# Narrowing a float64 weight tile by tile: w_out of block 0 by itself, and w_out two blocks behind gate and val

## The chip, the cores and the metric

The kernel runs on one core of a Trainium2 chip. The metric is the time of one execution on the device in microseconds, as the median of three executions. Every time below is in microseconds (us), unless it is marked ns.

## The reference

Two stages stand one behind the other. The first is an attention with a polynomial sketch, for 4 batches of 4 heads with 1088 tokens of 32 values. Its output, 4352 tokens of 128 values, is the input of a gated feed-forward layer.

```python
def phi(x):                                   # S1, S2: 8 x 32
    a = np.einsum('rd,bhsd->bhsr', S1, x)
    b = np.einsum('rd,bhsd->bhsr', S2, x)
    return np.einsum('bhsi,bhsj->bhsij', a, b).reshape(*x.shape[:-1], r * r)
q_p, k_p = (phi(q), phi(k))
kv = np.einsum('bhsf,bhsd->bhfd', k_p, v)
z = np.sum(k_p, axis=2)
num = np.einsum('bhsf,bhfd->bhsd', q_p, kv)
den = np.einsum('bhsf,bhf->bhs', q_p, z)[..., None] + 1e-06
attn = num / den
...                                           # x: (4352, 128), from attn
gate = 1.0 / (1.0 + np.exp(-(x @ w_gate)))    # w_gate, w_val: 128 x 1536
val = x @ w_val
out = (gate * val) @ w_out                    # w_out: 1536 x 128
```

S1, S2, w_gate, w_val and w_out reach the kernel as 64-bit floats; q, k and v are 32-bit floats.

## The kernel before

The hidden size of 1536 is worked in 12 blocks of 128 (`NJ = 12`), and the tokens in 9 chunks (eight of 512 and one of 256). For each chunk and block TensorE makes a *wave* (gate and val of the block, two products), ScalarE the sigmoid `sg`, VectorE the product `g`, and TensorE adds `w_out.T @ g` of the block into `moeout`. The products of w_out run two blocks behind the waves.

TensorE takes 32-bit floats, so each 64-bit weight is *narrowed* first. It arrives as two 32-bit words, and one part of the weights goes through four steps that are shared out over three engines, each step being called by its number (0 to 3) from where it is wanted in the program:

```python
def narrow(out, bits, eng, bank=None, copies=None):
    ...
    # step 0: GpSimd (eng) and ScalarE read the raw words
    eng.tensor_scalar(out=cap.bitcast(F32), in0=hi.bitcast(F32), scalar1=122880.0, scalar2=-122880.0,
                      op0=ALU.min, op1=ALU.max)
    nc.scalar.activation(out=tail, in_=lo, func=ACTF.Copy, scale=2.0**-29)
    yield
    # step 1: VectorE, two instructions
    nc.vector.tensor_scalar(out=head, in0=cap, ...)
    nc.vector.scalar_tensor_tensor(out=head, in0=cap, ..., in1=head, ...)
    yield
    # step 2: ScalarE and GpSimd
    square = ...                      # in a bank of PSUM ("acc0" or "acc1"), or over cap
    nc.scalar.activation(out=square, in_=cap.bitcast(F32), func=ACTF.Square)
    nc.gpsimd.tensor_tensor(out=head, in0=head, in1=tail, op=ALU.add)
    yield
    # step 3: VectorE writes the 32-bit weights
    nc.vector.scalar_tensor_tensor(out=out, in0=square, ..., in1=head, op0=ALU.is_ge, op1=MUL)
    yield
```

The raw words come in by loads on SyncE's queue, all of them issued at the head of the program, in this order and with the loads of q and v between:

```python
load_w_in(0, 1)                       # gate and val of block 0
v_t[0] = load_v(0)
load_w_in(1, 2)                       # gate and val of block 1
load_w_out(0)                         # w_out of blocks 0 and 1
load_rows(q, 0, q_t[0], ((T0, T, nc.sync),))
for n in range(1, NJ // 2):
    load_w_in(2 * n, 2 * n + 2)       # gate, then val, of blocks 2n and 2n+1
    load_w_out(n)                     # w_out of blocks 2n and 2n+1
```

The raw words of each pair of blocks have a tile of their own (`raw` has six of them, `[P, 3, 2, P, 2]`: gate, val, w_out; two blocks; 128 weights; two words). The parts are: gate and val of block 0; gate and val of block 1; w_out of blocks 0 and 1; and from block 2 on gate, val and w_out of one block together.

```python
for part in range(2):
    narrow_01(part, 0)                # gate and val of blocks 0 and 1: step 0
...
def rest(turn, rc, dT):               # on the way to the first tokens x
    kv0([1, 2, 3, 4, 0])
    ...
    turn()
    nc.scalar.activation(out=rc[:, :nt], in_=dT[:, :nt, :2], func=ACTF.Identity, bias=eps)
    kvd(0)
    narrow_01(0, 1)
    narrow_01(0, 2)
    ndt(0)
divide = dn(0, 0, rest)
warm(256)                             # products of constants, of no use but to keep TensorE at work
def head1():
    narrow_01(1, 1)
    narrow_01(0, 3)
    narrow_01(1, 2)
    narrow_01(2, 0)                   # w_out of blocks 0 and 1
    narrow_w(2, 0)                    # gate, val and w_out of block 2
divide((0, 4), (4, 8), between=head1)
narrow_01(1, 3)
narrow_01(2, 1)
narrow_01(2, 2)
```

The rest of the parts is called from within the waves of the first chunk (`ci == 0`), two blocks ahead:

```python
nc.scalar.activation(out=sg, in_=wv[:, 0], func=ACTF.Sigmoid)
if ci == 0:
    if j0 == 1:
        narrow_01(2, 3)
    if 0 < j0 < NJ - 2:
        narrow_w(j0 + 1, 3)
    narrow_w(j0 + 2, 1)
    narrow_w(j0 + 2, 2)
    if j0 < 3:
        narrow_w(j0 + 3, 0)
    if j0 > 1:
        narrow_w(j0 + 4, 0)
```

In the loop over the waves the product of w_out of block j - 2 stands right ahead of wave j:

```python
while len(todo) >= lag:               # lag is 2
    w2(*todo.pop(0))                  # moeout += w_out.T @ g, of block j - 2
if more:
    w1()                              # the wave of block j
```

Of the kernel before, what the change touches and what calls it, by code (L numbers as in the profile page):

```python
# [8 lines left out]
F32 = mybir.dt.float32  # L9
I32 = mybir.dt.int32  # L10
# [6 lines left out]
P = 128  # L17
# [3 lines left out]
def kernel(  # L21
# [12 lines left out]
    nc = tc.nc  # L34
# [6 lines left out]
    NJ = DFF // P  # L41
# [10 lines left out]
    const = ctx.enter_context(tc.tile_pool(name="const", bufs=1))  # L52
    ld = ctx.enter_context(tc.tile_pool(name="ld", bufs=1))
    sbA = ctx.enter_context(tc.tile_pool(name="sbA", bufs=2))
    raw = ctx.enter_context(tc.tile_pool(name="raw", bufs=NJ // 2))
    sbN = ctx.enter_context(tc.tile_pool(name="sbN", bufs=1))
    sbG = ctx.enter_context(tc.tile_pool(name="sbG", bufs=6))

# [21 lines left out]
    wide = S1.dtype == I64  # L80
# [61 lines left out]
                nc.sync.dma_start(out=rows, in_=s_)  # L142


    w_sb = const.tile([P, 3, NJ, P], F32, tag="w_sb", name="w_sb")
    w_in = {}

    def load_w_in(j0, j1):
        cs = slice(j0 * P, j1 * P)
        n, jj = divmod(j0, 2)  # L150
        if wide and jj == 0:
            w_in[n] = raw.tile([P, 3, 2, P, 2], I32, tag="w_in", name="w_in")
        for i, src in enumerate((moe_w_gate, moe_w_val)):
            if wide:
                nc.sync.dma_start(  # L155
                    out=w_in[n][:, i, jj : jj + j1 - j0].rearrange("p j m w -> p (j m w)"),
                    in_=src[:, cs].bitcast(I32),
                )
            else:
                nc.sync.dma_start(  # L160
                    out=w_sb[:, i, j0:j1].rearrange("p j m -> p (j m)"), in_=src[:, cs]
                )

    def load_w_out(n):
        j0, j1 = 2 * n, 2 * n + 2
        cs = slice(j0 * P, j1 * P)
        src = moe_w_out[cs, :].bitcast(I32) if wide else moe_w_out[cs, :]
        nc.sync.dma_start(
            out=w_in[n][:, 2].rearrange("p j m w -> p j (m w)") if wide else w_sb[:, 2, j0:j1],
            in_=src.rearrange("(j p) m -> p j m", p=P),  # L170
        )

    narrowing = {}

    def narrow_w(j, step):
        if not 0 <= j < NJ:
            return
        n, jj = divmod(j, 2)
        if wide:
            if step == 0:  # L180
                narrowing[j] = narrow(
                    w_sb[:, :, j, :], w_in[n][:, :, jj], nc.gpsimd, "acc1" if j < NJ - 2 else None
                )
            next(narrowing[j])


    def narrow_01(part, step):
        if wide:
            if step == 0:
                i = (slice(0, 2), part) if part < 2 else (2, slice(0, 2))  # L190
                narrowing["01", part] = narrow(
                    w_sb[:, i[0], i[1]],
                    w_in[0][:, i[0], i[1]],
                    nc.gpsimd,
                    "acc0" if part else "acc1",
                )
            next(narrowing["01", part])


    def load_rows(src, b, t, parts=((0, T, nc.sync),)):  # L200
# [76 lines left out]
    for c in range(2):  # L277
        rows = slice(64 * c, 64 * c + 64)
        nc.vector.tensor_reduce(
            out=m_col[rows, c],  # L280
            in_=ident[rows].rearrange("p (k j) -> p j k", j=R),
# [3 lines left out]
    for t, x in (  # L285
# [5 lines left out]
        out=e_sum,  # L291
        in_=bass.AP(
            tensor=e_row.tensor,
            offset=e_row.offset,
            ap=[list(e_row.ap[0]), [0, 2], [1, R], [0, R]],
        ),
# [13 lines left out]
    def w2(ci, j0, jn, g):  # L310
        t0, tw = tok_chk[ci]
        if j0 == 0:
            moe["sum"] = ci
            moe["acc"] = pso.tile([P, TCH], F32, tag=f"acc{ci % 2}", name="moeout")
        for jj in range(jn):
            j = j0 + jj
            nc.tensor.matmul(  # L317
                out=moe["acc"][:, :tw],
                lhsT=w_sb[:, 2, j, :],
                rhs=g[:, jj, :tw],  # L320
                start=(j == 0),
                stop=(j == NJ - 1),
            )
        if j0 + jn == NJ:
            o_sb = sbA.tile([P, TCH // 32, 32], F32, tag="o_sb", name="o_sb")
            nt = tw // 32
            nc.vector.transpose(  # L327
                out=o_sb[:, :nt, :].rearrange("p t d -> p (t d)"), in_=moe["acc"][:, :tw]
            )
            c = t0  # L330
            while c < t0 + tw:
                b, r = divmod(c, S)
                n = min(t0 + tw - c, S - r) // 32
                u = (c - t0) // 32
                for g4 in range(4):
# [12 lines left out]
    def w1():  # L348

        ci = moe["ci"]  # L350
        t0, tw = tok_chk[ci]
        jn = TCH // tw
        j0 = moe["w"] * jn
        wv = psm.tile([P, 2, TCH], F32, tag="wave", name="wave")

        tp = tw // 2 if ci == 0 and j0 == 0 else tw
        for o in range(0, tw, tp):
            for which in range(2):
                for jj in range(jn):
                    nc.tensor.matmul(  # L360
                        out=wv[:, which, jj * tw + o : jj * tw + o + tp],
                        lhsT=w_sb[:, which, j0 + jj, :],
                        rhs=xT[:, t0 + o : t0 + o + tp],
                        start=True,
                        stop=True,
                    )
        sg = sbG.tile([P, TCH], F32, tag="sg", name="sg", bufs=3)
        nc.scalar.activation(out=sg, in_=wv[:, 0], func=ACTF.Sigmoid)  # L368
        if ci == 0:
            if j0 == 1:  # L370
                narrow_01(2, 3)
            if 0 < j0 < NJ - 2:
                narrow_w(j0 + 1, 3)
            narrow_w(j0 + 2, 1)
            narrow_w(j0 + 2, 2)
            if j0 < 3:
                narrow_w(j0 + 3, 0)
            if j0 > 1:
                narrow_w(j0 + 4, 0)


        def glu():
            g = sbG.tile([P, TCH], F32, tag="g", name="g")
            nc.vector.tensor_tensor(out=g, in0=wv[:, 1], in1=sg, op=MUL)  # L384
            moe["todo"].append((ci, j0, jn, g.rearrange("p (j t) -> p j t", j=jn)))

        moe["gate"] = glu
        moe["w"] += 1
        if j0 + jn == NJ:
            moe["ci"] += 1  # L390
            moe["w"] = 0
# [140 lines left out]
    def outer(b, pi, j0=0, j1=NJK, eng=nc.vector):  # L532
        a0 = KAB[b][:, pi, j0:j1]
        ap = [list(a0.ap[0]), [2 * R, 2 * (j1 - j0)]]
        eng.tensor_tensor(  # L535
            out=KP[b][:, pi, j0:j1].rearrange("p j m (i l) -> p (j m) i l", i=R),
            in0=bass.AP(tensor=a0.tensor, offset=a0.offset, ap=ap + [[1, R], [0, R]]),
            in1=bass.AP(tensor=a0.tensor, offset=a0.offset + R, ap=ap + [[0, R], [1, R]]),
            op=MUL,
        )  # L540
# [257 lines left out]
    else:  # L798
        nc.vector.tensor_copy(
            out=s4[:, 1:],  # L800
            in_=bass.AP(
                tensor=s4.tensor, offset=s4.offset, ap=[list(s4.ap[0]), [0, 3], [1, D]]
            ),
# [5 lines left out]
        out=st_[:, : 2 * R],  # L809
        lhsT=s4.rearrange("p g d -> p (g d)"),  # L810
# [9 lines left out]
        out=sk,  # L820
# [13 lines left out]
    for n, inner in enumerate(([[1, R], [0, R]], [[0, R], [1, R]])):  # L834
# [3 lines left out]
            out=t, in_=bass.AP(tensor=s0.tensor, offset=s0.offset, ap=[list(s0.ap[0])] + inner)  # L838
# [9 lines left out]
    mult10 = ab(None, (0, 1, 0), (psm, "wave"))  # L848
    for pi in range(2):
        outer(0, pi, NJK - 1, NJK, eng=nc.gpsimd)  # L850
    for part in range(2):
        narrow_01(part, 0)
    spread_z()
    warm(512)
    for pi in range(2):
# [6 lines left out]
    def rest(turn, rc, dT):  # L862
        kv0([1, 2, 3, 4, 0])
        for pi in range(2):
            outer(0, pi, 5, NJK - 1)
        kv0(range(5, NJK))
        turn()
        nt = rc.shape[1] - 1
        nc.scalar.activation(out=rc[:, :nt], in_=dT[:, :nt, :2], func=ACTF.Identity, bias=eps)
        kvd(0)  # L870
        narrow_01(0, 1)
        narrow_01(0, 2)
        ndt(0)

    divide = dn(0, 0, rest)
    warm(256)

    def head1():
        narrow_01(1, 1)
        narrow_01(0, 3)  # L880
        narrow_01(1, 2)
        narrow_01(2, 0)
        narrow_w(2, 0)

    divide((0, 4), (4, 8), between=head1)
    narrow_01(1, 3)
    narrow_01(2, 1)
    narrow_01(2, 2)

    slot(None, 1)  # L890
    cq = {}
# [82 lines left out]
```

## Time and profile before

The median is 305.58 us, of executions between 305.27 and 306.23. The profiled execution has a span of 303.6 us at a granted TensorE clock of 0.998. By stage:

| stretch, us | what runs | TensorE busy, us | VectorE | ScalarE | GpSimd | DMA, GB/s |
|---|---|---|---|---|---|---|
| 0 to 15.20 | attention of the first tokens | 13.14 | 12.38 | 6.61 | 4.93 | 286 |
| 15.20 to 50.57 | first chunk, parts 2 to 11 narrowed | 34.86 | 30.44 | 16.77 | 17.04 | 146 |
| 50.57 to 283.50 | the other chunks, attention between | 232.93 | 106.27 | 54.02 | 13.33 | 57 |
| 283.50 to 303.60 | last chunks, output | 16.41 | 5.73 | 3.58 | 0.00 | 21 |

How to read the profile's lines: `PE` is TensorE's products and `PEld` its loads of weights, `DVE` is VectorE, `ACT` ScalarE, `POOL` GpSimd and `SP` SyncE; a `q` behind an engine's name is its queue, which issues and waits. `L127` is line 127 of the kernel, and `w_sb<-square,head` reads: written from. Several lines of the profile are lines of helpers: L97 and L101 are step 0 of a narrowing (`cap` and `tail`), L105 and L109 step 1 (`head`), L117 and L118 step 2 (`square`, and the add into `head`), L127 step 3 (`w_sb`). L360 is the wave, L317 the product of w_out, L155 the load of w_gate and w_val, L168 that of w_out. An end of a product is modelled: back to back, one of 512 columns has a pass every 0.429 us, and its record is some 0.16 us longer.

### The profile page before, as it was taken

How to read it: one execution, taken by the hardware profiler on the slowest of the kernel's cores; microseconds unless marked ns; L12 is line 12 of the kernel's file. 1: busy time of each engine (PE TensorE's matmuls, PEld its weight loads, DVE VectorE, ACT ScalarE, POOL GpSimd, SP SyncE). 2: the span in 40 equal slices, each digit the busy share in tenths (PEclk: the TensorE clock that was granted, in tenths of full speed). 3: DMA queues.
4: the chain of work that ended last, by engine and by line, in shares of the span. 5: the costliest groups of instructions: out<-in, count | busy, mean ns of one | idle time of the engine just before them, and what ended most of it. 6: DMA issues, size and time to landing. Idle time of an engine off the chain costs nothing.

```text
span 303.6 us, 3618 instructions
## 1 busy us (share of the span) xinstructions
PE 297.3 (98%) x1366; PEld 136.9 (45%) x1366; DVE 154.8 (51%) x266; ACT 81.0 (27%) x150; POOL 35.3 (12%) x65
## 2 busy tenths in 40 slices
PE   8899999999999999999999999999999999999995
PEld 3444433454344444433444445334444444444683
DVE  6997788756556444464365443635232223222331
ACT  2556532221222222221222222221222222222220
POOL 1465540600000500000005000000000000000000
PEclk9999999999999999999999999999999999999999
DMA  7992440897202593440016930200010000100011
GB/s 219 354 341 68 124 144 6 174 182 181 74 9 56 92 174 56 94 169 0 0 18 129 174 64 2 36 2 0 0 23 11 0 0 9 28 0 0 7 31 17
DMA packets 29874, 23.31 MB, mean 77 GB/s; under 512 B 20960, under 2 KB 25056, under 8 KB 29856
## 3 DMA queue, kind: packets, MB, share of 16 engines
q1 hardware_dynamic: 25488, 15.21, 18.5%
q0 software_dynamic: 3456, 7.09, 13.6%
q10 hardware_dynamic: 912, 0.77, 0.9%
q8 instruction: 11, 0.18, 0.2%
q14 instruction: 7, 0.06, 0.1%
HBM read 19.80 MB, written 3.26 MB: 76 GB/s over the span
## 4 chain that ended last, share of the span: by engine, by line
PE 84%; DMA 7%; DVE 4%; POOL 3%; issue 1%; SPq 1%; ACT 0%; POOLq 0%; ACTq 0%
PE wave L360 52%; PE moeout L317 27%; DMA v<-in_v_dram 3%; POOL head L118 3%; DMA w_in<-in_moe_w_out_dram 2%; DMA w_in<-in_moe_w_gate_dram 2%; DVE w_sb L127 1%; DVE head L109 1%; PE kvz L657 1%; PE nps L754 1%; PE dps L735 1%; DVE head L105 1%; PE kps L456 1%; PE cqps L602 0%; SPq L155 0%
## 5 line engine op out<-in xcount | busy, mean ns | idle before, releaser
L360 PE MATMUL wave<-xT,w_sb 128*128 128x512 f32 (+1 forms) x436 | 191.7, 565 | 0.1
L384 DVE TENSOR_TENSOR g<-wave,sg 128x512 f32<-128x512 f32 x102 | 70.3, 689 | 130.1 <-ACT sg L368 129.8
L360 PEld LDWEIGHTS wave<-xT,w_sb 128*128 128x128 f32 x436 | 82.6, 190 | 93.6 <-issue 86.3
L368 ACT ACTIVATE sg<-wave 128x512 f32<-128x512 f32 x102 | 60.9, 597 | 199.0 <-PE wave L360 199.0
L317 PE MATMUL moeout<-g,w_sb 128*128 128x512 f32 (+1 forms) x216 | 105.4, 576 | 0.3 <-DVE w_sb L127 0.3
L317 PEld LDWEIGHTS moeout<-g,w_sb 128*128 128x128 f32 x216 | 39.5, 190 | 43.9 <-issue 37.1
L626 POOL DMA_DIRECT2D qp<-dq x12 | 7.1, 590 | 109.1 <-DMA dq<-cq 67.5
L118 POOL TENSOR_TENSOR head<-head,tail 128x384 int32<-128x384 int32 (+2 forms) x14 | 13.4, 954 | 17.8 <-DVE head L109 14.7
L535 DVE TENSOR_TENSOR kp<-kab 128x1152 f32<-128x1152 f32 (+2 forms) x10 | 10.5, 1069 | 0.0
L635 DVE TENSOR_TENSOR qp<-qp,bq 128x1152 f32<-128x1152 f32 (+1 forms) x7 | 9.1, 1293 | 1.1 <-DMA bq<-dq 1.1
L258 PE MATMUL warm<-const-float32-1.0 128*128 128x512 f32 (+1 forms) x12 | 7.2, 724 | 0.8 <-PEq L958 0.8
L109 DVE SCALAR_TENSOR_TENSOR head<-cap,head 128x384 int32<-128x384 int32 (+2 forms) x14 | 7.5, 535 | 0.5
L127 DVE SCALAR_TENSOR_TENSOR w_sb<-square,head 128x384 f32<-128x384 f32 (+1 forms) x11 | 5.7, 518 | 3.9 <-POOL head L118 3.9
L327 DVE STREAM_TRANSPOSE o_sb<-moeout 128x512 f32<-128x512 f32 (+1 forms) x9 | 6.1, 680 | 2.6 <-PE moeout L317 2.5
L626 POOL DMA_DIRECT2D bq<-dq x12 | 7.0, 579 | 0.3
L101 ACT ACTIVATE tail<-w_in 128x384 int32<-128x384 uint32 (+1 forms) x13 | 6.5, 517 | 0.5 <-DMA w_in<-in_moe_w_gate_dram 0.5
L97 POOL TENSOR_SCALAR cap<-w_in 128x384 f32<-128x384 f32 (+1 forms) x13 | 6.5, 504 | 0.0
L781 DVE TENSOR_TENSOR xT<-nps,rb 128x576 f32<-128x576 f32 (+2 forms) x9 | 5.9, 661 | 0.7
L770 DVE STREAM_TRANSPOSE rb<-rc 128x576 f32<-128x576 f32 (+2 forms) x9 | 6.1, 680 | 0.3
L754 PE MATMUL nps<-qp,nd 64*32 64x256 f32 (+1 forms) x128 | 5.5, 401 | 0.4 <-ACT nd L726 0.4
L439 DVE STREAM_TRANSPOSE qT<-kq 128x512 f32<-128x512 f32 (+1 forms) x8 | 5.7, 718 | 0.0
L117 ACT ACTIVATE square<-cap 128x384 f32<-128x384 f32 (+1 forms) x11 | 5.1, 463 | 1.9 <-DVE w_sb L127 1.8
(73 smaller groups left out, 84.6 us busy)
## 6 DMA issues: line engine op xcount, KB each, us to landing
qp<-dq POOLq DMA_DIRECT2D x12, 288.0 KB, 9.3
bq<-dq POOLq DMA_DIRECT2D x12, 288.0 KB, 9.6
v<-in_v_dram SPq DMA_DIRECT2D x16, 144.0 KB, 6.1
kq<-in_k_dram SPq DMA_DIRECT2D x3, 544.0 KB, 4.0
kq<-in_q_dram SPq DMA_DIRECT2D x3, 544.0 KB, 4.9
w_in<-in_moe_w_out_dram SPq DMA_DIRECT2D x6, 256.0 KB, 6.9
w_in<-in_moe_w_gate_dram SPq DMA_DIRECT2D x5, 256.0 KB, 5.7
w_in<-in_moe_w_val_dram SPq DMA_DIRECT2D x5, 256.0 KB, 4.8
```

Source lines behind the costliest of these rows:

```text
L109: nc.vector.scalar_tensor_tensor(out=head, in0=cap, scalar=-0x40000000, in1=head, op0=ALU.bitwise_and, op1=ALU.bitwise_or)
L118: nc.gpsimd.tensor_tensor(out=head, in0=head, in1=tail, op=ALU.add)
L127: nc.vector.scalar_tensor_tensor(out=out, in0=square, scalar=1.265625 * 2.0**-30, in1=head, op0=ALU.is_ge, op1=MUL)
L258: nc.tensor.matmul(out=t[:, 0, :n], lhsT=x, rhs=r, start=True, stop=True)
L317: nc.tensor.matmul(out=moe["acc"][:, :tw], lhsT=w_sb[:, 2, j, :], rhs=g[:, jj, :tw], start=(j == 0), stop=(j == NJ - 1),)
L360: nc.tensor.matmul(out=wv[:, which, jj * tw + o : jj * tw + o + tp], lhsT=w_sb[:, which, j0 + jj, :], rhs=xT[:, t0 + o : t0 + o + tp], sta ...
L368: nc.scalar.activation(out=sg, in_=wv[:, 0], func=ACTF.Sigmoid)
L384: nc.vector.tensor_tensor(out=g, in0=wv[:, 1], in1=sg, op=MUL)
L535: eng.tensor_tensor(out=KP[b][:, pi, j0:j1].rearrange("p j m (i l) -> p (j m) i l", i=R), in0=bass.AP(tensor=a0.tensor, offset=a0.offset, ...
L626: get.dma_start(out=t[64 * c : 64 * c + 64, n * H * W1 : (n + 1) * H * W1], in_=bass.AP(tensor=d0.tensor, offset=d0.offset, ap=rows + [[1, ...
L635: nc.vector.tensor_tensor(out=q0, in0=q0, in1=half(BQ[b], n), op=MUL)
L754: nc.tensor.matmul(out=t[32 * h : 32 * h + 32, c, :w], lhsT=ND[b][rows, 32 * h : 32 * h + 32], rhs=half(QP[b], n)[rows, 2 * (h % 2) + h // ...
```

## The change

The change aims at the first products of w_out: they need only w_out of block 0, but that is narrowed together with w_out of block 1, and gate and val of block 2 together with a w_out that is not needed until later. So w_out of block 0, and gate and val of block 2, become parts of their own; from block 3 on a part holds gate and val of block j with w_out of block j - 2; and one last part holds w_out of blocks 10 and 11. For a part to be one access with a fixed step, the raw words of all blocks lie in one tile: gate of blocks 0 to 11 on places 0 to 11, val on 12 to 23, two empty places, and w_out on 26 to 37. A part of block j takes places j, j + 12 and j + 24. The 32-bit weights `w_sb` lie in the same way. Loads, their order and their sizes stay.

```diff
-    raw = ctx.enter_context(tc.tile_pool(name="raw", bufs=NJ // 2))
+    raw = ctx.enter_context(tc.tile_pool(name="raw", bufs=1))
...
-    w_sb = const.tile([P, 3, NJ, P], F32, tag="w_sb", name="w_sb")
-    w_in = {}
+    w_sb = const.tile([P, 3 * NJ + 2, P], F32, tag="w_sb", name="w_sb")
+    w_in = raw.tile([P, 3 * NJ + 2, P, 2], I32, tag="w_in", name="w_in") if wide else None
...
-                    out=w_in[n][:, i, jj : jj + j1 - j0].rearrange("p j m w -> p (j m w)"),
+                    out=w_in[:, i * NJ + j0 : i * NJ + j1].rearrange("p j m w -> p (j m w)"),
...
+        to = slice(2 * NJ + 2 + j0, 2 * NJ + 2 + j1)
...
-            out=w_in[n][:, 2].rearrange("p j m w -> p j (m w)") if wide else w_sb[:, 2, j0:j1],
+            out=w_in[:, to].rearrange("p j m w -> p j (m w)") if wide else w_sb[:, to],
...
+    def narrow_w(part, step):
+        if wide and part in places:
             if step == 0:
-                narrowing[j] = narrow(
-                    w_sb[:, :, j, :], w_in[n][:, :, jj], nc.gpsimd, "acc1" if j < NJ - 2 else None
-                )
...
+                at, bank = places[part]
+                narrowing[part] = narrow(w_sb[:, at], w_in[:, at], nc.gpsimd, bank)
+            next(narrowing[part])
+
+    places = {j: (slice(j, j + 2 * NJ + 1, NJ), "acc1") for j in range(3, NJ - 2)}
+    places.update({j: (slice(j, j + 2 * NJ + 1, NJ), None) for j in range(NJ - 2, NJ)})
+    places.update({("gv", j): (slice(j, j + NJ + 1, NJ), f"acc{1 - j % 2}") for j in range(3)})
+    places["out", 0] = slice(2 * NJ + 2, 2 * NJ + 3), "acc0"
+    places[NJ] = slice(3 * NJ, 3 * NJ + 2), None
...
-                lhsT=w_sb[:, 2, j, :],
+                lhsT=w_sb[:, 2 * NJ + 2 + j, :],
...
         if ci == 0:
-            if j0 == 1:
-                narrow_01(2, 3)
-            if 0 < j0 < NJ - 2:
-                narrow_w(j0 + 1, 3)
-            narrow_w(j0 + 2, 1)
-            narrow_w(j0 + 2, 2)
+            if j0 == 0:
+                narrow_w(("gv", 2), 1)
+                narrow_w(("gv", 2), 2)
+                narrow_w(("out", 0), 3)
+            else:
+                if j0 == 1:
+                    narrow_w(("gv", 2), 3)
+                elif j0 != NJ - 2:
+                    narrow_w(j0 + 1, 3)
+                narrow_w(j0 + 2, 1)
+                narrow_w(j0 + 2, 2)
...
     def head1():
-        narrow_01(1, 1)
-        narrow_01(0, 3)
-        narrow_01(1, 2)
-        narrow_01(2, 0)
-        narrow_w(2, 0)
+        narrow_w(("gv", 1), 1)
+        narrow_w(("gv", 0), 3)
+        narrow_w(("gv", 1), 2)
+        narrow_w(("out", 0), 0)
+        narrow_w(("gv", 2), 0)
...
-    narrow_01(1, 3)
-    narrow_01(2, 1)
-    narrow_01(2, 2)
+    narrow_w(("gv", 1), 3)
+    narrow_w(("out", 0), 1)
+    narrow_w(("out", 0), 2)
```

More of the change, by code (lines that the diff above doesn't have):

```diff
@@ L142, in load_s @@
                 nc.sync.dma_start(out=rows, in_=s_)
-    w_sb = const.tile([P, 3, NJ, P], F32, tag="w_sb", name="w_sb")
-    w_in = {}
+    w_sb = const.tile([P, 3 * NJ + 2, P], F32, tag="w_sb", name="w_sb")
+    w_in = raw.tile([P, 3 * NJ + 2, P, 2], I32, tag="w_in", name="w_in") if wide else None
     def load_w_in(j0, j1):
         cs = slice(j0 * P, j1 * P)
-        n, jj = divmod(j0, 2)
-        if wide and jj == 0:
-            w_in[n] = raw.tile([P, 3, 2, P, 2], I32, tag="w_in", name="w_in")
         for i, src in enumerate((moe_w_gate, moe_w_val)):
@@ L160, in load_w_in @@
                 nc.sync.dma_start(
-                    out=w_sb[:, i, j0:j1].rearrange("p j m -> p (j m)"), in_=src[:, cs]
+                    out=w_sb[:, i * NJ + j0 : i * NJ + j1].rearrange("p j m -> p (j m)"),
+                    in_=src[:, cs],
                 )
@@ L173 @@
     narrowing = {}
[L175 to L179, printed above, removed]
-            if step == 0:
-                narrowing[j] = narrow(
-                    w_sb[:, :, j, :], w_in[n][:, :, jj], nc.gpsimd, "acc1" if j < NJ - 2 else None
-                )
[L184 to L197, printed above, removed]
+    def narrow_w(part, step):
+        if wide and part in places:
+            if step == 0:
+                at, bank = places[part]
[6 more added lines that the diff above has]
+    places[NJ] = slice(3 * NJ, 3 * NJ + 2), None
     def load_rows(src, b, t, parts=((0, T, nc.sync),)):
@@ L361, in w1 @@
                         out=wv[:, which, jj * tw + o : jj * tw + o + tp],
-                        lhsT=w_sb[:, which, j0 + jj, :],
+                        lhsT=w_sb[:, which * NJ + j0 + jj, :],
                         rhs=xT[:, t0 + o : t0 + o + tp],
@@ L850 @@
         outer(0, pi, NJK - 1, NJK, eng=nc.gpsimd)
-    for part in range(2):
-        narrow_01(part, 0)
+    narrow_w(("gv", 0), 0)
+    narrow_w(("gv", 1), 0)
     spread_z()
@@ L870, in rest @@
         kvd(0)
-        narrow_01(0, 1)
-        narrow_01(0, 2)
+        narrow_w(("gv", 0), 1)
+        narrow_w(("gv", 0), 2)
         ndt(0)
```

## The prediction

> **What bounds the kernel now.** I began with the page's busy shares and its table of 40 slices, to see whether any engine but TensorE could set the end:
>
> ```profile
> PE 297.3 (98%) x1366; PEld 136.9 (45%) x1366; DVE 154.8 (51%) x266; ACT 81.0 (27%) x150; POOL 35.3 (12%) x65
> ...
> PE   8899999999999999999999999999999999999995
> ```
>
> TensorE is busy for 297.3 of 303.6 us. A saving can lie only where it idles, which is before about 50 us; a loss can come from whatever holds it up there. The list of waits, TensorE's alone from 15 us on, has one entry:
>
> ```profile
> PE moeout L317 <- DVE w_sb L127: 0.3, 1, 0.3
> ```
>
> The timeline shows where this wait stands and what surrounds it (columns: start, us, engine, line, operation, out<-in, idle before and its releaser):
>
> ```profile
> 15.20 3.71 PE L360 MATMUL wave<-xT,w_sb 128*128 128x256 f32 x12
> ...
> 18.79 0.41 DVE L127 SCALAR_TENSOR_TENSOR w_sb<-square,head 128x256 f32<-128x256 f32 x1
> ...
> 19.25 1.12 PE L317 MATMUL moeout<-g,w_sb 128*128 128x512 f32 x2 [0.34 <-DVE w_sb L127]
> ```
>
> The waves of blocks 0 and 1 are issued from 15.20 to 18.63 (eight passes of 256 columns and four of 512, at the steady 0.429 us per 512), but the first w_out product starts at 19.25, because w_out of blocks 0 and 1 is finished at 19.20. So 0.6 us is lost. This is what the change aims at.
>
> Then I looked at what lets narrowing start at all: the first caps on GpSimd, the issue of the weight loads on SyncE, and SyncE's waits.
>
> ```profile
> 10.07 0.78 POOL L97 TENSOR_SCALAR cap<-w_in 128x256 f32<-128x256 f32 x2
> ```
> ```profile
> 12.43 0.72 SPq L155 DMA_DIRECT2D w_in<-in_moe_w_gate_dram  x1
> ...
> 15.81 0.33 SPq L155 DMA_DIRECT2D w_in<-in_moe_w_gate_dram  x1
> ```
> ```profile
> SPq L626 <- DMA w_in<-in_moe_w_gate_dram: 1.3, 1, 1.3
> ```
> ```profile
> L626 SPq EVENT_SEMAPHORE  x2: 17/17/17, 21.6 to 28.0; - x2
> ```
>
> Blocks 0 and 1 begin to be narrowed at 10.07 us, as soon as their own loads are in. The last load of w_gate (blocks 10 and 11) is issued only at 15.81, and SyncE, after its last v issue ended at 20.35, waits 1.3 us for that load and goes on at 21.6. So **the last gate load lands at 21.6 us**.
>
> **What the Trainium skill says.** *DMA: Bandwidth & Descriptors*, "Why a DMA increments its semaphore by 16 and not by 1": only the full 16 of a DMA says that its data has landed. In the changed program as built, GpSimd's first cap and ScalarE's first tail wait for six DMA semaphores instead of three. One is awaited at 64: the fourth DMA on that semaphore, which is the load of gate blocks 10 and 11. *TensorE: Matmul & The Clock Gate*, "What's actually happening": after an idle window of about 3.4 us the array runs at half clock, until a window of activity has passed. The trace agrees as to the start: the first weight loads of `warm` take 0.34 us each (to 4.33 us), and those at 5.53 take 0.35 for two. No idle stretch that long is in the trace of before. *SBUF — State Buffer*, "SBUF: two separate sides": VectorE and GpSimd lock a shared port pair against each other. The trace agrees: head of block 2 (17.26) takes 1.01 us instead of 0.56, and it ends 0.42 after GpSimd's add does.
>
> **The change, part by part.**
>
> (1) *One tile for the raw weights.* Before, six tiles held a pair of blocks each. Now one tile holds gate 0..11, val 0..11, two empty places and w_out 0..11, and a part takes its places with a stride of 12. The first part takes places 0 and 12, and the waits as built cover every load between them: gate blocks 1 to 11. The order of the loads is unchanged, so 10.07 becomes 21.6. GpSimd and ScalarE run in order, so all behind the first cap and tail waits too: ScalarE's reciprocal input, kvd and nd, hence the `ndps` and `nps` products and xT.
>
> Restart from T = 21.6, with durations of before: two tails on ScalarE 0.81, rc 0.31, kvd 0.27: T+1.4. The transpose on TensorE 0.33 and nd 0.27, with hand-overs: T+2.1. `nps` to T+2.8. VectorE meanwhile: head of part 0 blocked by the second cap to T+0.9, head's second step 0.43, reciprocal and rb to T+2.0, head of part 1 blocked by GpSimd's add to T+2.4, second step to T+2.9, w_sb (overlapping by 0.08) to T+3.2, first xT to T+3.6. First wave at T+3.65 = 25.25 instead of 15.20: **+10.1**.
>
> (2) *The cold array.* TensorE's kvz ends at 12.9 and nothing follows before T+1.4 = 23.0: ten idle us. `nps` and the 256-column `warm` (0.59 + 0.43 at full clock) at half clock put the first wave at up to T+4.2; as VectorE gave T+3.65, I take **+0.4**. At the program's start the half clock lasted from 0.78 to about 5; here it starts at 23.0 with thin activity, so I estimate it to last to 27 to 29, that is 1.5 to 3.5 us into the waves, of which half is lost: **+1.3**.
>
> (3) *The smaller parts.* w_out of block 0 alone has 128 columns instead of 256, gate and val of block 2 256 instead of 384. A step of VectorE falls by 0.10 to 0.13 per 128 columns (0.43 to 0.56, 0.25 to 0.35), GpSimd's add by 0.28 (0.73 to 1.0). Chained from 15.88 of before: head of w_out 0 ends 16.75, its add 17.35, w_sb 17.9, g of block 0 18.56, so the first w_out product goes at 18.65 instead of 19.25: **-0.6**; w_sb of block 3 comes 1.0 earlier.
>
> (4) *w_out of block j-2 in part j.* Before, wave j waited for part j; now the w_out product of j-2, which stands 0.86 ahead of wave j, does. Part j ended this long before wave j: 0.43 (block 5), 0.37, 0.33, 0.27, 0.23 (block 9). The parts come every 2.62 (w_sb 0.56, head 0.28 and 0.57, hand-over 0.19, add 1.0), TensorE's blocks every 2.575. Margin at block 9: 0.23 + (1.0 - 0.66) - 0.86 = -0.3; TensorE waits, and of 0.66 gained 0.25 is left. Part 11 (w_sb ends 46.03 before) is met again one product earlier, and what is gained at `nps` (qp no longer late) is paid there: **+0.45**, net -0.15.
>
> (5) *A thirteenth part* (w_out 10 and 11, 256 columns): VectorE 0.25 + 0.43 + 0.42, GpSimd and ScalarE as much, off TensorE's path but for g of block 10, whose margin was 0.6: **0**. From 50 us on TensorE is gapless and all is merely later.
>
> Sum: 305.6 + 10.1 + 0.4 + 1.3 - 0.6 + 0.45 = **317.2**.
>
> **Rivals.** *A: the intended gain alone*: the first cap still starts near 10. For it: the operands of the first part touch only early loads. Against it: the waits as built. It would give 305.4. *B: a wait on an earlier load only*, that of gate 8 and 9: issued at 12.43, and at about 6 us from issue to landing (the page has 5.7 for w_gate, 6.9 for w_out) in at 18.5, so 3.1 us less: 314. Against it: the count of 64 on the semaphore of blocks 10 and 11. *C: no cold array*: T alone counts, 315.5; for it, `warm` and `nps` run before the waves; against it, ten idle us. *D: a longer half clock*, to 31 or 32: the chain of g, sg and parts stretches with TensorE, 319.5.
>
> **Range and chances.** The first term is ten times all others, and its spread is that of a landing (0.5 either way). The cold array gives 0 to 3.5, the parts 0.5. I predict **317.2 us**, 8 times in 10 between 315.0 and 319.6. Slower by over 2% (311.7) needs only 6 us of the 10: 0.95; within 2%: 0.035; faster: 0.015.
>
> **What would show it.** The first `cap` and `tail` of w_in at 21.6, released by the DMA of w_gate; TensorE's slices from 13 to 23 us nearly empty; the first wave between 25 and 26; weight loads of 0.34 us for the first few us of waves; no wait of `moeout` for block 0; then short waits of `moeout` on w_sb around blocks 5 to 11. If the first cap starts before 19, the main term is wrong; if the first waves' weight loads take 0.19, the second is.

## The result, and the profile after

| | before | after |
|---|---|---|
| time, median (us) | 305.43 (305.27 to 306.23, 4 runs) | 317.31 (316.49 to 318.05, 4 runs) |
| ratio to before | 1 | 1.0383 (95%: 1.0348 to 1.0417) |
| span of the profiled execution | 303.6 | 316.0 |

The change costs 11.9 us; 317.2 was predicted. The page of after has its busy shares and slices (one slice is 7.9 us) like this:

```profile
PE 299.8 (95%) x1366; PEld 138.0 (44%) x1366; DVE 155.8 (49%) x269; ACT 80.8 (26%) x152; POOL 35.7 (11%) x67
PE   8509999999999999999999999999999999999995
PEclk9956999999999999999999999999999999999999
```

TensorE does the same 1366 products. What is new stands in the second to fourth digits: TensorE half busy, then not at all (the granted clock falls to 0.5 there), and then busy at a granted clock of 0.6. From there on all is as full as before. The waits, TensorE's two that are new or changed and SyncE's for the last load of gate:

```profile
PE ndps L709 <- ACT kvd L675: 9.9, 1, 9.9
PE moeout L308 <- DVE w_sb L127: 0.7, 2, 0.5
```
```profile
SPq L622 <- DMA w_in<-in_moe_w_gate_dram: 1.3, 1, 1.3
```

One wait of 9.9 us for ScalarE's copy `kvd` holds nearly the whole loss. `kvd` itself is a copy of 0.24 us; why it is late is seen one step further back, in the timeline:

```profile
15.48 0.33 SPq L153 DMA_DIRECT2D w_in<-in_moe_w_gate_dram  x1
...
21.48 0.75 ACT L101 ACTIVATE tail<-w_in 128x256 int32<-128x256 uint32 x2 [12.81 <-DMA w_in<-in_moe_w_out_dram]
21.58 0.78 POOL L97 TENSOR_SCALAR cap<-w_in 128x256 f32<-128x256 f32 x2 [11.63 <-DMA v<-in_v_dram]
...
22.63 0.47 PE L709 MATMUL ndps<-ident,kvd 128*128 128x128 f32 x1 [9.87 <-ACT kvd L675]
...
25.51 5.23 PE L351 MATMUL wave<-xT,w_sb 128*128 128x256 f32 x12
30.57 1.02 PE L308 MATMUL moeout<-g,w_sb 128*128 128x512 f32 x2
...
57.04 1.12 PE L308 MATMUL moeout<-g,w_sb 128*128 128x512 f32 x2 [0.53 <-DVE w_sb L127]
...
60.09 1.13 PE L308 MATMUL moeout<-g,w_sb 128*128 128x512 f32 x2 [0.20 <-DVE w_sb L127]
```

The first cap and tail, those of block 0, start at 21.5 after GpSimd and ScalarE have idled for 11.6 and 12.8 us, although they need only words that were there early: in before, with the same order of loads, the first cap starts at 10.07. `kvd` stands behind the tail in ScalarE's program: the last product of `kvz`, which it copies, ends at 12.76, and it runs at 22.33, after tail and `rc`. The releasers in the brackets (a load of w_out, one of v) are put there by the profile, which takes what came last before the start: neither belongs to block 0's gate and val, nor lies between them in the tile. SyncE's own wait for the last gate load ended at 21.3 (the issue of v ends at 20.00, then 1.3), which fits.

How much later each landmark is than in before tells where the time comes from (starts of TensorE's products):

| landmark | before | after | later by |
|---|---|---|---|
| first wave | 15.20 | 25.51 | 10.3 |
| first w_out product | 19.25 | 30.57 | 11.3 |
| wave of block 3 | 23.61 | 34.82 | 11.2 |
| wave of block 9 | 39.06 | 50.59 | 11.5 |
| w_out product of block 9 | 44.96 | 57.04 | 12.1 |
| first wave of chunk 1 | 48.76 | 61.05 | 12.3 |
| last w_out product of the trace | 299.53 | 311.82 | 12.3 |

After chunk 1 begins, the lag of every product stays at 12.3 to the end. So there are three questions: the 10.3 us ahead of the first wave, the 1.0 us in the first waves, and the 1.0 us between the first w_out product and chunk 1, where the change was meant to gain.

### The profile page after: what moved, and what is told of

Read it like the earlier page. It is cut to its first block, busy times and chain, and to the rows that moved or that the text cites. A ratio compares the mean times of both kernels' runs of the same rounds, so it can differ in the third digit from the quotient of the medians.

```text
span 316.0 us, 3624 instructions
## 1 busy us (share of the span) xinstructions
PE 299.8 (95%) x1366; PEld 138.0 (44%) x1366; DVE 155.8 (49%) x269; ACT 80.8 (26%) x152; POOL 35.7 (11%) x67
## 4 chain that ended last, share of the span: by engine, by line
PE 88%; DMA 6%; DVE 2%; POOL 1%; ACT 1%; issue 1%; SPq 0%; ACTq 0%
PE wave L351 54%; PE moeout L308 28%; DMA w_in<-in_moe_w_val_dram 2%; DMA w_in<-in_moe_w_gate_dram 2%; PE nps L750 2%; DMA v<-in_v_dram 1%; PE kvz L653 1%; PE dps L731 1%; DMA kq<-in_k_dram 1%; POOL head L118 1%; PE cqps L598 1%; PE kps L452 1%; DVE w_sb L127 0%; PE warm L249 0%; PE ndps L709 0%
## 5 line engine op out<-in xcount | busy, mean ns | idle before, releaser
L351 PEld LDWEIGHTS wave<-xT,w_sb 128*128 128x128 f32 x436 | 84.1, 193 | 93.4 <-issue 89.2
L118 POOL TENSOR_TENSOR head<-head,tail 128x384 int32<-128x384 int32 (+3 forms) x15 | 13.6, 904 | 21.2 <-DVE head L109 10.0
L709 PE MATMUL ndps<-ident,kvd 128*128 128x128 f32 x7 | 1.6, 301 | 9.9 <-ACT kvd L675 9.9
L531 DVE TENSOR_TENSOR kp<-kab 128x1152 f32<-128x1152 f32 (+2 forms) x10 | 10.5, 1069 | 0.0
L105 DVE TENSOR_SCALAR head<-cap 128x384 int32<-128x384 int32 (+3 forms) x15 | 5.4, 360 | 10.0 <-POOL cap L97 9.9
L101 ACT ACTIVATE tail<-w_in 128x384 int32<-128x384 uint32 (+2 forms) x14 | 6.7, 499 | 12.8 <-DMA w_in<-in_moe_w_out_dram 12.8
L97 POOL TENSOR_SCALAR cap<-w_in 128x384 f32<-128x384 f32 (+2 forms) x14 | 6.7, 488 | 11.6 <-DMA v<-in_v_dram 11.6
L109 DVE SCALAR_TENSOR_TENSOR head<-cap,head 128x384 int32<-128x384 int32 (+3 forms) x15 | 7.4, 496 | 0.5
L127 DVE SCALAR_TENSOR_TENSOR w_sb<-square,head 128x384 f32<-128x384 f32 (+2 forms) x11 | 5.4, 493 | 2.8 <-POOL head L118 2.8
```

Source lines behind the costliest of these rows:

```text
L109: nc.vector.scalar_tensor_tensor(out=head, in0=cap, scalar=-0x40000000, in1=head, op0=ALU.bitwise_and, op1=ALU.bitwise_or)
L351: nc.tensor.matmul(out=wv[:, which, jj * tw + o : jj * tw + o + tp], lhsT=w_sb[:, which * NJ + j0 + jj, :], rhs=xT[:, t0 + o : t0 + o + tp ...
L531: eng.tensor_tensor(out=KP[b][:, pi, j0:j1].rearrange("p j m (i l) -> p (j m) i l", i=R), in0=bass.AP(tensor=a0.tensor, offset=a0.offset, ...
```

## Experiments

### The layout: one tile, or the order of the parts?

Theory: the parts of the change are innocent; the loss comes from putting all raw words into one tile, in which a part with a stride of 12 makes its first step wait for all loads that lie between its first and last place. Two kernels take the change apart. The first keeps its parts, and the new layout of `w_sb`, and puts the raw words back into a tile for each pair of blocks, with w_out of a pair in the next tile:

```diff
-    w_in = raw.tile([P, 3 * NJ + 2, P, 2], I32, tag="w_in", name="w_in") if wide else None
+    w_in = {}
...
+    def raw_of(n):
+        if n not in w_in:
+            rows = 2 if n == 0 else 1 if n == NJ // 2 else 3
+            w_in[n] = raw.tile([P, rows, 2, P, 2], I32, tag=f"w_in{n}", name="w_in")
+        return w_in[n]
...
-                narrowing[part] = narrow(w_sb[:, at], w_in[:, at], nc.gpsimd, bank)
+                narrowing[part] = narrow(w_sb[:, at], raw_part(part), nc.gpsimd, bank)
```

> The new parts (w_out of block 0 alone, gate and val of block 2 alone, w_out two blocks behind) with the raw words in tiles of one pair of blocks, as in the kernel before, so that each part waits only for its own loads. Theory (the one raw tile makes the first part wait for the last gate load, the new parts cost little): first cap near 10 us, first wave near 15.2, 305.3 us, between 305.0 and 305.8. Rival 1 (the new parts cost most of it: w_out waits and the thirteenth part, 1.0 us in the trace of the changed kernel): 306.4. Rival 2 (the raw tile is not the cause at all): about 317.

Measured: 306.21 us (305.51 to 307.12), ratio 1.0018 (1.0010 to 1.0027). The second keeps the parts of before and takes only the one tile:

```diff
-            w_in[n] = raw.tile([P, 3, 2, P, 2], I32, tag="w_in", name="w_in")
+    w_in = raw.tile([P, 3, NJ, P, 2], I32, tag="w_in", name="w_in")
...
-                    w_sb[:, :, j, :], w_in[n][:, :, jj], nc.gpsimd, "acc1" if j < NJ - 2 else None
+                    w_sb[:, :, j, :], w_in[:, :, j], nc.gpsimd, "acc1" if j < NJ - 2 else None
```

> The kernel before, its parts unchanged, with the raw words of all blocks in one tile: the layout of the change alone. Theory: first cap at 21.5, released by the last gate load, and 316.6 to 317.4 us, nearly the whole loss. Rival (the loss comes with the new parts): 305.4.

Measured: 316.28 us (315.90 to 317.68), ratio 1.0357 (1.0338 to 1.0377). Its timeline has the same late first cap as after:

```profile
21.70 0.79 POOL L97 TENSOR_SCALAR cap<-w_in 128x256 f32<-128x256 f32 x2 [11.76 <-DMA v<-in_v_dram]
```

The layout alone makes 10.9 of the 11.9 us (the intervals of the two kernels overlap); the parts alone make 0.18%. Which load it is that the first part waits for is told by a kernel in which only the raw words of blocks 10 and 11 leave the tile. Ten blocks (`RJ`) are left in the tile, and the first part then spans the loads up to gate 8 and 9 only:

```diff
+    w_last = raw.tile([P, 3, 2, P, 2], I32, tag="w_last", name="w_last")
...
-                    out=w_in[:, i * NJ + j0 : i * NJ + j1].rearrange("p j m w -> p (j m w)"),
+                    out=(w_last[:, i] if j0 == RJ else w_in[:, i * RJ + j0 : i * RJ + j1]).rearrange("p j m w -> p (j m w)"),
```

> The changed kernel with the raw words of blocks 10 and 11 in a tile of their own, so that the first part waits for the load of gate 8 and 9 as its last, and not for 10 and 11. Theory (the time follows the landing of the last load covered): first cap near 18.8, 2.7 us earlier, 314.6 us. Rival (the first part waits for all loads of the weights, or for the queue to run dry): 317.3.

Measured: 314.55 us (313.73 to 315.45), ratio 1.0293 (1.0275 to 1.0311). In its timeline, the load of gate 8 and 9, the first cap and the first waves:

```profile
12.50 0.66 SPq L155 DMA_DIRECT2D w_in<-in_moe_w_gate_dram  x1
...
19.18 0.79 POOL L97 TENSOR_SCALAR cap<-w_in 128x256 f32<-128x256 f32 x2 [8.55 <-DMA w_last<-in_moe_w_out_dram]
...
23.16 4.01 PE L366 MATMUL wave<-xT,w_sb 128*128 128x256 f32 x12
```

The load on which the span ends was issued at 12.50 instead of 15.48, 3.0 us earlier; the cap starts 2.4 earlier, the first wave 2.35, and the time falls by 2.8. The cap follows the last load of its span, and not its own words. (The releaser named in the bracket is a load that no first part reads: once more it isn't the cause.)

### The cold array

The prediction gave 1.7 us to a TensorE that runs at half clock after its idle stretch. Two kernels keep it busy with products that nobody reads. The first puts ten of 512 columns in front of the waiting `ndps`:

```diff
+        warm(*[512] * 10)
```

> The changed kernel with ten more products of constants (512 columns, 0.86 us each) on TensorE in the stretch in which it idles from 12.8 to 22.6. They add no time of their own. Theory (the cold array costs 1.5 us in the first waves and 0.3 ahead of them): weight loads of the first waves 0.19 us instead of 0.39, 315.5 us, 1.8 less than the changed kernel. Rival (the first waves are slow for waits on VectorE's chain, not for the clock): 317.3, unchanged.

Measured: 317.02 us (316.30 to 317.91), ratio 1.0375 (1.0356 to 1.0393): as the rival said, nothing gained in the median. But the trace doesn't say what the rival says. The view of busy time by stretch (columns: stretch, its length, busy share of PE, PEld, DVE, ACT and POOL with the number of records, granted clock, busy share of the DMA engines, GB/s), for after and then for this kernel:

```profile
15.00:16.00 1.00, 0.00 (x0) 0.00 (x0) 0.00 (x0) 0.00 (x0) 0.00 (x0) 0.56 1.05 369
24.00:25.00 1.00, 1.00 (x17) 0.50 (x2) 0.96 (x3) 0.46 (x2) 0.40 (x1) 0.50 0.07 24
28.00:29.00 1.00, 1.00 (x4) 0.82 (x3) 0.00 (x0) 0.00 (x0) 1.00 (x2) 0.61 0.00 0
```
```profile
24.00:25.00 1.00, 1.00 (x18) 0.47 (x18) 0.96 (x3) 0.95 (x3) 0.53 (x1) 1.00 0.06 16
28.00:29.00 1.00, 1.00 (x4) 0.80 (x3) 0.51 (x2) 0.00 (x0) 0.55 (x2) 0.50 0.06 16
29.00:30.00 1.00, 1.00 (x3) 0.52 (x2) 0.05 (x1) 0.68 (x2) 0.69 (x2) 0.67 0.00 0
```

In after the clock is halved within the stretch 15 to 16 and comes back within 28 to 29: half clock over 13.65 us, waves included. With the ten products the clock is whole while `ndps` and `nps` run, and is then halved for 3.41 us, from 26.3 to 29.7, just when the waves have begun. The half clock came after 21.8 to 25.9, where TensorE had only `ndps`, `nps` and one product of 256 columns and waited in between. So in this execution warming had only moved the half clock onto the waves.

The four executions differ in this. One stretch of 3.41 us at half clock takes 0.005 from the mean granted clock. Two executions have 0.995 (the one of the trace) and 0.993, and took 317.91 and 317.45 us; the other two have 0.999 and 0.998, which leaves no room for it, and took 316.30 and 316.58. So the stretch of half clock goes with 1.2 us more (its place in the waves is known from the one trace only), and the median lies between the two kinds. A second kernel fills the thin stretch too:

```diff
+        warm(*[512] * 12)
...
-    warm(256)
+    warm(256, 256)
```

> The changed kernel with TensorE kept at work not only while it waits (as in e3, where the half clock fell on the first waves all the same, for one window of 3.41 us) but up to the first wave: twelve products of 512 columns ahead of ndps, and 256 columns more after nps. Theory (a window with little work in it cuts the clock, so e3 missed only the stretch of 21.5 to 25.8 us): no stretch of half clock, first twelve wave records in 3.7 us instead of 5.2 to 5.4, and 315.5 to 316.3 us. Rival (the clock falls after any such wait, or the slow waves have another cause): waves of 5.2 us again, 317.2.

Measured: 316.72 us (316.31 to 316.89), ratio 1.0363 (1.0349 to 1.0376). The page has the clock whole throughout, and the timeline the first waves:

```profile
PEclk9999999999999999999999999999999999999999
```
```profile
23.79 0.27 PE L709 MATMUL ndps<-ident,kvd 128*128 128x128 f32 x1
...
25.98 3.60 PE L351 MATMUL wave<-xT,w_sb 128*128 128x256 f32 x12
29.43 1.02 PE L308 MATMUL moeout<-g,w_sb 128*128 128x512 f32 x2
```

The first twelve wave records take 3.60 us instead of 5.23, which is 1.6 saved; 0.5 of it is paid back, since `ndps` now stands behind the last of the added products and the first wave comes at 25.98 instead of 25.51. The lag behind before is 11.2 at chunk 1 instead of 12.3. By the traces the cold array is worth 1.1 us net of the warming. The medians show 0.6, and the intervals of the two kernels overlap. But all four executions of this kernel (316.31 to 316.89) lie with the two of the first warming kernel that kept the clock, so the times bear the effect out: about 1.2 us for one stretch of half clock on the waves.

### The parts: where the intended gain goes

With a tile for each pair of blocks (the first kernel above) the change is 0.18% slower than before, where it should be faster. Its trace shows the gain and its loss. The first w_out product follows the waves without a wait. But from block 3 on the product is bound by its part (w_out of block 3 is written at 27.88, its product starts at 27.93), and at block 9 it waits:

```profile
45.87 1.12 PE L323 MATMUL moeout<-g,w_sb 128*128 128x512 f32 x2 [0.54 <-DVE w_sb L127]
```

Against before its w_out products stand at -0.08 us (block 0), -0.19 (blocks 1 and 2), +0.03 (3), +0.29 (7), +0.91 (9) and +0.75 (11), in a trace whose first wave was 0.42 later. (The trace is of the slowest execution, 307.12 us. It loses another 0.94 at 77 us, in the second chunk, where VectorE's `qp` has waited 4.03 for the transfer of `bq` and the product waits 0.67 for a `g` behind it. No part is waited for there, and whether the other executions have this isn't known; so how much of the 0.18% the parts make stays open.) Theory: w_out of block j-2 in part j sets the product of j-2, which stands 0.86 us ahead of wave j, as the bound; a lag of one block takes that away. So the next kernel has w_out of block j-1 in part j, and w_out of block 11 alone as the thirteenth part. Its loads of w_out are grouped to fit (block 0, then 1 and 2, and so on to 11 alone: seven instead of six), which the lines leave out:

```diff
-    places = {j: (slice(j, j + 2 * NJ + 1, NJ), "acc1") for j in range(3, NJ - 2)}
+    places = {j: (slice(j, j + 2 * NJ + 1, NJ), "acc1") for j in range(2, NJ - 2)}
...
-    places.update({("gv", j): (slice(j, j + NJ + 1, NJ), f"acc{1 - j % 2}") for j in range(3)})
-    places["out", 0] = slice(2 * NJ + 2, 2 * NJ + 3), "acc0"
-    places[NJ] = slice(3 * NJ, 3 * NJ + 2), None
+    places.update({("gv", j): (slice(j, j + NJ + 1, NJ), f"acc{1 - j % 2}") for j in range(2)})
+    places["out", 0] = slice(2 * NJ + 1, 2 * NJ + 2), "acc0"
+    places[NJ] = slice(3 * NJ, 3 * NJ + 1), None
```

> Tiles of pairs as in e1, w_out of block 0 alone, but w_out of block j-1 (not j-2) with gate and val of block j, so that the w_out product does not wait for a part ahead of the wave; the last part is w_out of block 11 alone. Theory (in e1 the 0.6 us gained at the first w_out product is lost again because the product of w_out j-2 now waits for part j, 0.86 us ahead of wave j, and because the thirteenth part delays part 11): 305.2, 0.8 to 1.0 under e1 and 0.3 under the kernel before. Rival (in e1 it is the extra part or the layout as such): 306, as e1.

Measured: 305.51 us (305.30 to 306.52), ratio 1.0004 (0.9996 to 1.0013): the same time as before, and by the medians 0.7 us under the lag of two (the two intervals just overlap). The products stand at a flat -0.19 from block 0 to block 7 although the first wave was 0.31 later in this trace, so the gain of 0.5 is there and is kept. It is lost at the end: -0.18 at block 9, -0.02 at block 10, +0.25 at block 11. Two reasons can be read around block 10:

```profile
41.62 0.36 POOL L97 TENSOR_SCALAR cap<-w_in 128x128 f32<-128x128 f32 x1
41.68 0.71 DVE L127 SCALAR_TENSOR_TENSOR w_sb<-cap,head 128x384 f32<-128x384 f32 x1 [0.30 <-POOL head L118]
...
46.06 1.98 PE L366 MATMUL wave<-xT,w_sb 128*128 128x512 f32 x4 [0.26 <-DVE w_sb L127]
```

VectorE's last step of part 10 takes 0.71 us beside GpSimd's cap of the thirteenth part (0.56 before). *SBUF — State Buffer*, "SBUF: two separate sides", of the Trainium skill has an operation of VectorE with two inputs in SBUF and one of GpSimd that reads SBUF lock a shared port pair against each other. The traces agree as to when it happens: parts 10 and 11 keep their square over `cap`, in SBUF, and the same step with its square in a bank of PSUM isn't slower beside a cap, as in before:

```profile
22.06 0.54 POOL L97 TENSOR_SCALAR cap<-w_in 128x384 f32<-128x384 f32 x1
22.13 0.56 DVE L127 SCALAR_TENSOR_TENSOR w_sb<-square,head 128x384 f32<-128x384 f32 x1
```

They don't show the whole of a lock: the step in question overlaps the cap by 0.30 us and is longer by 0.15. After it VectorE is busy without a gap up to wave 11, which now waits. The second reason: VectorE's steps of the thirteenth part stand at 46.6 to 48.1 ahead of the transposes of k of the next batch. One kernel moves the cap, the next the three steps as well:

```diff
+                if j0 == NJ - 2:
+                    narrow_w(NJ, 0)
...
-            if j0 > 1:
+            if j0 > 1 and j0 + 4 != NJ:
                 narrow_w(j0 + 4, 0)
```

> The variant with w_out of block j - 1 in part j and pair tiles, with one thing moved: GpSimd's cap of the thirteenth part comes after wave 10 instead of after wave 8. In the variant before it the cap stood at 41.62 us and the last step of part 10 took 0.71 us beside it against 0.56 in the kernel before. Theory (the two share a port to SBUF, and VectorE is full from 41.7 to 46.0 us): the last step of part 10 takes 0.56 again, every VectorE instruction up to wave 11 comes 0.15 us earlier, and the time is 305.35 us. Rival (VectorE isn't the bound there): wave 11 doesn't move, 305.5 us.

Measured: 305.40 us (305.26 to 307.01), ratio 1.0003 (0.9992 to 1.0013).

```diff
         turn_q(b, 0)
         slot(None, wn)
+        if b == 1:
+            narrow_w(NJ, 1)
+            narrow_w(NJ, 2)
         turn_q(b, 1)
+        if b == 1:
+            narrow_w(NJ, 3)
```

> As the late cap, and VectorE's three steps of the thirteenth part moved behind the transposes of k of the next batch: they are due only at the product of block 11, at 51.7 us, and the variant with lag one ran them at 46.6 to 48.1 us, which put those transposes 0.8 us later and the product of block 11 0.25 us later than in the kernel before, though its waves stood level. Theory (the thirteenth part's place on VectorE is what gives the gain of the first product back): waves of the second chunk 0.2 to 0.4 us earlier than in the kernel before, 305.0 us. Rival (VectorE has no gap there either, and whatever is moved delays the transposes of q): 305.5 us or more.

Measured: 305.94 us (305.16 to 308.38), ratio 1.0019 (1.0003 to 1.0036). With the late cap the last step of part 10 is back at 0.56 and wave 11 no longer waits:

```profile
41.31 0.56 DVE L127 SCALAR_TENSOR_TENSOR w_sb<-cap,head 128x384 f32<-128x384 f32 x1 [0.29 <-POOL head L118]
```

Both kernels hold their lead up to block 10 (-0.54 and -0.64 us) and lose 0.27 and 0.22 of it at the product of block 11, for two different reasons. With the late cap alone, VectorE's transposes of q for the next batch (`qT`) end 0.28 later than in before, behind the three steps of the thirteenth part, and the attention products `cqps`, which stand ahead of the product of block 11, start 0.74 after `kps` instead of 0.51:

```profile
49.88 0.76 DVE L452 STREAM_TRANSPOSE qT<-kq 128x576 f32<-128x576 f32 x1
...
50.78 0.72 PE L615 MATMUL cqps<-qT,skq 64*32 64x288 f32 x16
```

With the steps moved as well, `cqps` comes 0.51 after `kps` again, but the part itself is finished at 51.23, and the product of block 11 follows it at 51.28:

```profile
50.94 0.29 DVE L127 SCALAR_TENSOR_TENSOR w_sb<-cap,head 128x128 f32<-128x128 f32 x1 [0.75 <-ACT cap L117]
```

They keep -0.27 and -0.42 to the last product of the trace. The times don't show such a lead: the first equals before, and the second, whose trace is of one of its fastest executions (305.17), has an interval just above 1. So neither is faster, and by the traces the thirteenth part costs about 0.25 us at the product of block 11 in each place that was tried for it, and its cap 0.15 more where it stood.

### Another order on VectorE

If the loop of narrowing steps sets the rate, VectorE's step on the next part might go ahead of the last step of this one. Tried on before, and on the lag of one:

```diff
             if 0 < j0 < NJ - 2:
+                narrow_w(j0 + 2, 1)
                 narrow_w(j0 + 1, 3)
-            narrow_w(j0 + 2, 1)
             narrow_w(j0 + 2, 2)
```

(The lines are those of the first kernel. The second has the same order from block 2 on, and besides it the late cap, and the last step of part 11 ahead of the transposes of the second half of the tokens.)

> The kernel before with VectorE's first step of part j+2 ahead of the last step of part j+1, nothing else changed. Theory: the parts of blocks 3 to 9 end earlier, which moves TensorE nowhere but at the second attention product and at block 11, 0.2 to 0.4 us: 305.2. Rival (w_sb of block 2 comes 0.9 us later behind the head of block 3 and the locks cost more): 306.4.

> As e8, and VectorE's first step of part j+2 stands ahead of the last step of part j+1 from block 2 on, so that the chain of 2.62 us per part (w_sb, head, head, add) is broken up; the last step of part 11 stands ahead of the transposes of the second half of tokens; the thirteenth part begins later. Theory (the chain of parts is what TensorE waits for at blocks 5 to 11): no wait of TensorE for w_sb after block 2, 304.6 us. Rival (VectorE and GpSimd lock each other out of the shared port for longer, as head and add now fall together): 305.5 or more.

Measured: 306.49 us (306.18 to 306.89), ratio 1.0022 (0.9999 to 1.0046) on before, and 306.35 us (306.08 to 307.12), ratio 1.0032 (1.0020 to 1.0043) on the lag of one. The times are near the rivals', though the first interval just reaches 1. The trace of the first shows one half of its rival's reason, a later w_sb of block 2:

```profile
19.32 0.53 POOL L97 TENSOR_SCALAR cap<-w_in 128x384 f32<-128x384 f32 x1
19.88 0.36 DVE L105 TENSOR_SCALAR head<-cap 128x384 int32<-128x384 int32 x1 [0.76 <-POOL cap L97]
...
20.75 0.55 DVE L127 SCALAR_TENSOR_TENSOR w_sb<-square,head 128x384 f32<-128x384 f32 x1
...
21.36 1.98 PE L360 MATMUL wave<-xT,w_sb 128*128 128x512 f32 x4 [1.05 <-DVE w_sb L127]
```

VectorE's head stands first now and waits 0.76 us for a cap that GpSimd has only just started, and the part behind it, which was ready at 19.35, is written at 20.75, 1.3 us later than in before. TensorE waits 1.05 us for it. The order of before hides this latency behind the last step. The other half, dearer locks, doesn't show in this trace: from block 3 on the second step of `head` takes 0.56 us as in before. In the second kernel's trace w_sb of blocks 3 and 4 comes late in the same way, and TensorE loses 1.1 us by block 3; there a first step of `head` takes up to 0.61 instead of 0.35, but the products fall back no further where it does.

## Why the prediction was right, and where it was off

**(1) One tile: right.** +10.1 was predicted for the first wave from a landing at 21.6, with the cold array's +0.4 in the head 10.5; measured 10.3, with the first tail and cap at 21.5. (The waits as built are those for val of block 0 and for gate of blocks 2 to 11. Two of them, not one, stand at 64: gate 8 and 9, and gate 10 and 11. The argument doesn't hang on this.) The layout alone makes 10.9 us in time, undone it leaves 0.18%, and letting two blocks out of the tile moves cap and time by nearly what the earlier load gives (2.4 and 2.8 of 3.0). Rival B (a wait on gate 8 and 9 only, 314) became a kernel of its own and measured 314.55. Rival A fell with the first cap. One sign failed as it was put: the cap was to be "released by the DMA of w_gate", and the timeline names other loads.

**(2) The cold array: right in kind, and in size for the execution of the trace.** +1.3 in the first waves was predicted and 1.5 measured (twelve records in 5.23 us instead of 3.71). The half clock was to last to 27 to 29, and did to 28.8. It doesn't in every execution: the mean granted clock is 0.978 in the two slower ones (317.74 and 318.05), which is the 13.65 us of the trace, and 0.981 and 0.982 in the two faster (316.49 and 316.88), which is less. Rival C (no cold array) fell with the clock row and rival D (to 31) with it.

**(3) The smaller parts: right.** The first w_out product is no longer late; the wait of `moeout` for block 0 is gone. In after the -0.6 shows as lags of 10.3 and 1.5 that make only 11.3 together, 0.5 less than their sum; with a tile for each pair the same 0.5 is seen without the cold array.

**(4) w_out of j-2: right in mechanism, too small.** Up to block 9 a loss of 0.41 was predicted (from 0.66 to 0.25; its own margin of -0.3 gives 0.3), and the lag grows by 0.25 in after, 0.48 with pair tiles; a lag of one block removes it. The term for part 11 ("what is gained at `nps` is paid there", near 0) is the mis-sized one: the product of block 9 waits 0.53 and falls back by 0.7. Its w_sb stands at the end of a run of VectorE work without a gap, and that run had been made longer ahead of it by step (5).

**(5) The thirteenth part: the step that failed.** It was put at 0, because its VectorE time lay off TensorE's path. But its cap on GpSimd runs beside the last step of part 10 (0.78 us in after, 0.56 in before), which makes part 11, and with it the product of block 9, later; and the product of block 10, not its `g`, is what needs the part: it waits 0.20 for the part's own w_sb, finished at 60.02.

```profile
52.53 0.42 POOL L97 TENSOR_SCALAR cap<-w_in 128x256 f32<-128x256 f32 x1
52.59 0.78 DVE L127 SCALAR_TENSOR_TENSOR w_sb<-cap,head 128x384 f32<-128x384 f32 x1 [0.28 <-POOL head L118]
```

(4) and (5) together were to cost 0.45 from the first product to chunk 1 and cost 1.0 in the trace. That is hidden in the time by the run-to-run spread of after, 1.6 us, and by (1), ten times as large: the time was met because the large term was right, while the small ones were off by half a microsecond. That the median came within 0.1 us is luck: the terms make 11.65 us, the trace 12.3, and the median lies between executions with a longer and a shorter half clock. And it is the small terms that answer whether the change could pay at all: with the layout put right, lag two was 0.2% slower, and lag one made no difference.

## What to carry to other kernels

When raw data of many loads is joined into one tile, ask for each reader what its stride spans, not what it reads: here a first step that needs two places of 38 waited for the loads in between and took ten us from a kernel whose arithmetic hadn't changed. Then ask what else stands behind that first step on its engines, because the wait is handed on to work that has no part in it (here `kvd`, for which TensorE waited 9.9 us). And where a part is taken off one end of a pipeline, look at the other end, where the remainder has to be done by itself.

## What the runs showed of the hardware

- The half clock came in whole multiples of one length: 13.65 us in after, 10.24 with the one tile alone, 6.83 with the last pair apart, 3.41 with ten warm products, so 4, 3, 2 and 1 times 3.41. *TensorE: Matmul & The Clock Gate*, "What's actually happening", of the Trainium skill has a free-running window of 3413 ns; the length agrees. The first twelve wave records took 5.23, 4.60, 4.01 and 5.40 us in these four (3.71 in before), by how much of the half clock fell on them (3.3, 2.0, 0.8 and 3.4 us) and not by how long TensorE had been idle ahead of `ndps` (9.87, 10.00, 6.84 and 1.55).
- A stretch that isn't idle can be followed by half clock: with ten warm products TensorE worked on and off in the stretch ahead of 26.3 (`ndps` 0.33, `nps` 0.67, `warm` 0.70, first waves from 25.85), and the clock was halved all the same; two other executions of the same kernel kept it (0.999 and 0.998). How much activity is enough wasn't measured.
- VectorE's last step of 384 columns with both inputs in SBUF (part 10) took 0.71 to 0.80 us beside a GpSimd cap of 0.36 to 0.44, and 0.56 without (before, and the late cap). With its square in PSUM it took 0.56 beside caps of 0.52 to 0.60.
